# Attention of two heads in pairs of PSUM banks, with new priorities

## The chip, the cores and the metric

One core of a Trainium2 chip. The metric is the device time in microseconds of one execution; the shown figure before is the median of three runs, 772.94 us. PE is TensorE, DVE VectorE, ACT ScalarE, POOL GpSimd, SP SyncE, whose queue issues all the transfers. PSUM, into which PE writes, has eight banks of 512 float32 columns.

## What is computed

Attention over 4 batches of 8 heads, 576 positions of 64 numbers, in two parts that are added: a coarse one (q, k and v averaged over four positions) and a local one (each position sees those less than four away). Then two feed-forward layers over the 4 x 576 tokens of 512 numbers. Cut from the reference:

```python
q_d, k_d, v_d = (t.reshape(B, H, S // 4, 4, D).mean(axis=3) for t in (q, k, v))
out_up = np.repeat(sm_attn(q_d, k_d, v_d), 4, axis=2)
mask = np.abs(pos[:, None] - pos[None, :]) < 4
out_local = softmax(where(mask, q @ k.T / 8, -1e9)) @ v
x = (out_up + out_local)                      # [B, S, 512]
xk, xr = mu_k * x + (1 - mu_k) * x_prev, mu_r * x + (1 - mu_r) * x_prev
x = sigmoid(xr @ w_r) * ((relu(xk @ w_k) ** 2) @ w_v)
x = x + relu(layernorm(x) * g_ln @ w_ch1) @ w_ch2
```

## The kernel before, in words

Attention goes by units: a unit is one batch and two neighbouring heads, 16 in all, four for a batch. Both heads lie one under the other in the 128 partitions (64 each), so that a unit gives 128 features of the array xT, from which the first layer reads. The function `attention(n, T0, TL)` adds a unit's operations to a list:

- Loads of k, q and v on SP's queue (`kin`, `qin`, `vw`, `v4`); q and k are transposed on DVE or, in units with a mode other than 0, on PE (`tq`) with an evacuation by ACT. `qd`, `kd`, `vd` are sums over four positions.
- Local scores `sc` (L623, L629): for each of the two heads one matmul that writes the mask into a bank, then 24 small matmuls (64 rows, 32 columns of the array; the trace shows two instructions for each). The head h lies in rows 64h to 64h+63. DVE takes the maximum (L640) and subtracts it (L643), ACT takes the exponential.
- Coarse scores `ds` (L655), in which the two heads alternate; their maximum on DVE, three exponentials on ACT.
- Sums, reciprocals and products on DVE; a 32x32 transpose to `pT` and four copies into the block matrix `PT`.
- `tp` (L707): six transposes of the coarse weights, in two tiles of one bank, each evacuated by ACT or DVE (L711, L712).
- `up` (L718): the coarse result, evacuated to `ups`.
- `pv` (L748): the local result in two halves of 288 positions, each a tile of one bank; DVE adds `ups` and writes xT (L762).

The first layer runs over six chunks of 384 tokens: `moe_r` (`psr`, sigmoid), `moe_k` (`psk`), `accumulate` (`psv`). The second runs over three pairs of chunks (`psh`, `pso`). Each float32 product is three matmuls (L778 to L780) of a high and a low part. The weights come as 64-bit numbers; two passes on ACT (L395, L397) and two on DVE (L402, L406) turn each 128x512 piece into float32, then a copy and a subtraction split it.

The order on each engine comes from the planner (`Plan.order`): all operations have a cost and a priority, and at every step it issues what can start earliest by its own simulation, the lower priority first among those. The priorities come from the table PRM. Where PE would stand before the first `psv`, the planner puts in warm-up matmuls (L433, tile `warm`) that compute nothing. A tile takes its bank when its first operation is issued and gives it back after its last. Tiles of one tag take turns in the order of their first operation.

Banks before: `ps_v` has three single banks (pv0, pv1, pv2; pv2 also holds the warm-ups), `ps_k` a ring of two, `ps_a` a ring of three. The function `psa` gives a bank to an attention tile: in batch 0 in turn from all three pools, later from the ring of three. In the second layer, `pso` uses all six of `ps_v` and `ps_a`.

A unit's work begins at priority T0, which for the first four is ta + u0 x n + t_n; loads of q and k have T0 - ld, loads of v ldv more. Loads of weights have the priority of their conversion less wld; for w_r that is wr + wrs x kt, for the first half of w_k wka + wkas x kt (kt from 0 to 3).

Of the kernel before, what the change touches and what calls it, by code (L numbers as in the profile page):

```python
# [9 lines left out]
F32 = mybir.dt.float32  # L10
# [14 lines left out]
    thin=89.915, t0=-16.294, t1=-9.875, t2=6.158, t3=7.667, t4=48.796, t5=19.99, t6=6.382, t7=-23.592, t8=-0.47,  # L25
    t9=-5.238, t10=-2.702, t11=0.12, t12=5.747, t13=-8.176, t14=-15.681, t15=-4.758, m0=2, m1=1, m2=0, m3=3, m4=1,
    m5=0, m6=0, m7=2, m8=3, m9=0, m10=0, m11=0, m12=0, m13=0, m14=0, m15=0, g0=0, g1=0, g2=0, g3=0, g4=0, g5=0, g6=0,
    g7=0, g8=0, g9=0, g10=0, g11=0, g12=0, g13=0, g14=0, g15=0, h0=1, h1=1, h2=1, h3=1, h4=0, h5=0, h6=0, h7=0, h8=0,
    h9=0, h10=0, h11=0, h12=0, h13=0, h14=0, h15=0, dve=0.27, pool=0, ta=-14.632, u0=4.274, tl=26.492, tm=4222.228,
    ld=33.163, ldv=76.41, mu=-14.605, wr=-0.059, wrs=-31.134, wka=-33.615, wkas=7.94, wkb=12.502, wkbs=-165.286,  # L30
    wv=103.601, wvs=2.875, wld=0.932, d0=235.165, d1=108.349, d2=260.708, d3=463.399, d4=581.694, d5=82886.056,
    a1=13.725, a1s=43.62, a1l=52.7, a2=-1.632, a2s=26.831, a2l=56.61, a3=54.215, a3s=40.382, a3l=96.628, xr=-60.685,
    xrs=16.307, xk=22.171, xks=1.12, xrn=9, xrns=1.512, xkn=-4.695, xkns=17.37, w2a=10.707, w2as=1.55, w2=7.281,
    w2s=34.846, wc=10.079, wcs=106.739, m2q=8, sld=-6.173, x1=3, wcg=-39.001, p0l=11.872, p0=2.352, p0s=3.263,
    p0n=7.723, dp=684.729, ra0=-8.097, ra1=-1.757, ra2=3.642, ra3=4.616, ra4=-5.44, ra5=0, rb0=0.342, rb1=19.209,
    rb2=16.653, rb3=33.463, rb4=10.116, rb5=0, rx0=-2.918, rx1=-13.421, rx2=8.601, rx3=12.062, rx4=-2.926, rx5=5.409,
    ne=12, we=52.842, wes=25.704, wel=6.378,
# [23 lines left out]
class Plan:  # L61
# [61 lines left out]
    def order(self):  # L123
# [17 lines left out]
        for k in sorted(range(nb), key=lambda k: first[k], reverse=True):  # L141
            turn[tag[k]].append(k)
# [123 lines left out]
def attn_moe_kernel(  # L266
# [175 lines left out]
    n_ps = [0]  # L442

    def psa(b, name):
        if b > 0:
            return Buf(ps_a, [P, 512], F32, "pa", 3, name)
        ring = [(ps_a, "pa", 3), (ps_k, "pk", 2), (ps_v, "pv0", 1), (ps_a, "pa", 3), (ps_k, "pk", 2),
                (ps_a, "pa", 3), (ps_v, "pv1", 1)]
        pool, tag, n = ring[n_ps[0] % len(ring)]
        n_ps[0] += 1  # L450
        return Buf(pool, [P, 512], F32, tag, n, name)

    def attention(n, T0, TL):
# [19 lines left out]
        join = PRM[f"g{n}"]  # L473
# [143 lines left out]
        for h in range(2):  # L617
            sc = psa(b, "sc")

            def score(h=h, sc=sc):  # L620
                if first:
                    warm_up(2)
                nc.tensor.matmul(sc()[:, :G * 32], identb, maskb.rearrange("p g c -> p (g c)"),  # L623
                                 start=True, stop=False)
                for g in range(G):
                    for j in range(4):
                        i = 4 * g + j
                        m = min(32, S - QB * i)
                        nc.tensor.matmul(  # L629
                            sc()[32 * j:32 * j + m, 32 * g:32 * g + 32],  # L630
# [5 lines left out]
            add("PE", 0.8 + hold(2), pr(0.2), score, r=[qT, kT], w=[sc] + held, thin=True)  # L636
            mx = Buf(at, [P, G, 1], F32, "mx", 2)
# [60 lines left out]


        pdT = Buf(at, [HS, 2, 2, SD], F32, "pdT", 1)  # L700
        for kt in range(2):
            tp = psa(b, "tp")
            tpv = lambda tp=tp: tp()[:HS, :2 * SD].rearrange("p (h c) -> p h c", c=SD)

# [598 lines left out]
```

## Time and profile before

| | us |
|---|---|
| runs (3) | 769.48, 772.94, 774.14 |
| median | 772.94 |
| the profiled execution | 771.95 |
| its span, first to last instruction | 770.2 |
| PE busy | 753.6 (98%) |
| DVE busy | 524.6 (68%) |
| ACT busy | 398.2 (52%) |

The granted clock of PE is 0.999 of full speed over the whole span. A busy PE in this table counts overlapping matmuls once, and counts warm-ups as well. Busy shares are means over stages with different limits, so the kernel is to be read by stage: 0 to 57 us (attention of batch 0, up to the first product), 57 to 235 us (attention of the batches 1 to 3 between products of the first layer), 235 to 387 us (first layer), 387 us to the end (second layer).

### The profile page before, as it was taken

What the parts mean: (1) busy time and instruction counts of PE and PEld (TensorE: products, weight loads), DVE (VectorE), ACT (ScalarE), POOL (GpSimd) and SP (SyncE); (2) the same over time, 40 slices, a digit from 0 to 9 for tenths busy, and PEclk for the clock granted to TensorE, in tenths of its full rate; (3) what the DMA queues carried; (4) which work ended last, traced back from release to release, by engine and by line L of the source; (5) the groups of instructions that cost most, each with busy time, mean ns of one, the idle gap of its engine ahead of it and who ended that gap; (6) DMA issues with size and microseconds to landing.
All of it is one profiled execution on the core that took longest, in us unless ns stands there. A gap on an engine that the chain in (4) does not pass through costs nothing.

```text
span 770.2 us, 15665 instructions
## 1 busy us (share of the span) xinstructions
PE 753.6 (98%) x5816; PEld 650.2 (84%) x5816; DVE 524.6 (68%) x1083; ACT 398.2 (52%) x916; POOL 63.8 (8%) x113
## 2 busy tenths in 40 slices
PE   9999999999999999999999999999999999999997
PEld 6878787788788798888888888889889899889886
DVE  6899999998985959878889763486543364333233
ACT  6889997987884847868835431221421131111110
POOL 3101122112100000000110000020000020000000
PEclk9999999999999999999999999999999999999999
DMA  8997596867768895964689894379853347443322
GB/s 190 208 192 180 180 180 124 182 170 144 207 159 267 251 323 171 290 217 135 141 281 289 208 258 121 112 246 305 183 150 115 112 121 258 138 120 113 123 69 82
DMA packets 202854, 140.88 MB, mean 183 GB/s; under 512 B 127120, under 2 KB 160028, under 8 KB 202780
## 3 DMA queue, kind: packets, MB, share of 16 engines
q1 hardware_dynamic: 202780, 139.90, 66.6%
q8 instruction: 46, 0.75, 0.4%
q14 instruction: 28, 0.23, 0.1%
HBM read 107.88 MB, written 31.98 MB: 182 GB/s over the span
## 4 chain that ended last, share of the span: by engine, by line
PE 77%; DVE 10%; DMA 6%; ACT 4%; issue 2%; POOL 0%; SPq 0%; DVEq 0%; POOLq 0%; ACTq 0%
PE pso L779 8%; PE pso L778 8%; PE pso L780 8%; PE psh L778 7%; PE psh L779 7%; PE psh L780 7%; PE psk L778 4%; PE psv L778 4%; PE psk L780 3%; PE psk L779 3%; PE psv L779 3%; PE psv L780 3%; DMA w<-in_moe_w_ch_dram 3%; PE warm L433 2%; DVE tmu L802 1%
## 5 line engine op out<-in xcount | busy, mean ns | idle before, releaser
L778 PE MATMUL psh<-xn,sa 128*128 128x384 f32 x336 | 114.0, 339 | 2.4 <-DVE c L1114 1.2
L779 PE MATMUL psh<-xn,sa 128*128 128x384 f32 x336 | 113.6, 338 | 0.0
L780 PE MATMUL psh<-xn,sa 128*128 128x384 f32 x336 | 113.3, 337 | 0.0
L778 PEld LDWEIGHTS psh<-xn,sa 128*128 128x128 f32 x336 | 63.1, 188 | 11.0 <-DVE c L1114 2.1
L779 PEld LDWEIGHTS psh<-xn,sa 128*128 128x128 f32 x336 | 63.1, 188 | 6.1 <-DVE xn L1051 0.2
L780 PEld LDWEIGHTS psh<-xn,sa 128*128 128x128 f32 x336 | 63.1, 188 | 0.0
L379 ACT ACTIVATE c22h<-t 128x384 fp32r<-128x384 f32 x24 | 12.6, 525 | 83.7 <-DVE t L1106 78.6
L395 ACT ACTIVATE wf<-w 128x512 f32<-128x512 f32 x48 | 32.3, 673 | 17.4 <-DMA w<-in_moe_w_ch_dram 9.2
L402 DVE SCALAR_TENSOR_TENSOR wf<-wf,w 128x512 uint32<-128x512 uint32 x48 | 32.9, 687 | 11.1 <-ACT w L397 10.6
L379 ACT ACTIVATE kr<-psk 128x384 f32<-128x384 f32 x46 | 22.4, 488 | 25.2 <-PE psk L780 21.2
L379 ACT ACTIVATE c11h<-psh 128x384 fp32r<-128x384 f32 x23 | 11.3, 491 | 45.8 <-PE psh L780 45.7
L397 ACT ACTIVATE w<-w 128x512 uint32<-128x512 uint8 x52 | 35.0, 672 | 0.0
L843 DVE TENSOR_TENSOR kl<-kr,kh 128x384 fp32r<-128x384 f32 x43 | 23.8, 553 | 14.6 <-ACT kr L842 14.3
L1083 DVE SCALAR_TENSOR_TENSOR c11l<-psh,c11h 128x384 fp32r<-128x384 f32 x24 | 13.3, 554 | 29.1 <-ACT c11h L379 29.1
L802 DVE SCALAR_TENSOR_TENSOR tmu<-xT,oms,tmu 128x384 f32<-128x384 f32 (+1 forms) x64 | 31.7, 512 | 1.8 <-ACT tmu L796 1.8
L406 DVE SCALAR_TENSOR_TENSOR wf<-w,wf 128x512 uint32<-128x512 uint32 x48 | 32.7, 680 | 0.3
L1106 DVE TENSOR_TENSOR t<-psh,t 128x384 f32<-128x384 f32 x24 | 13.3, 554 | 28.5 <-PE psh L780 28.4
L1097 DVE TENSOR_TENSOR u<-psh,u 128x384 f32<-128x384 f32 x24 | 13.3, 555 | 27.2 <-PE psh L780 27.1
L379 ACT ACTIVATE c12h<-c 128x384 fp32r<-128x384 f32 x24 | 12.6, 525 | 37.0 <-DVE c L1110 36.9
L379 ACT ACTIVATE c21h<-c 128x384 fp32r<-128x384 f32 x24 | 12.6, 523 | 34.6 <-DVE c L1114 34.6
L796 ACT ACTIVATE tmu<-xT,vecs 128x384 f32<-128x384 f32 (+1 forms) x51 | 26.8, 539 | 6.9 <-DVE xrl L806 4.0
L1103 DVE TENSOR_TENSOR t<-psh,u 128x384 f32<-128x384 f32 x24 | 13.2, 552 | 20.2 <-PE psh L780 20.1
(527 smaller groups left out, 2164.5 us busy)
## 6 DMA issues: line engine op xcount, KB each, us to landing
sa<-s_dram SPq DMA_DIRECT2D x168, 256.0 KB, 2.7
w<-in_moe_w_ch_dram SPq DMA_DIRECT2D x32, 512.0 KB, 6.2
s_dram<-s SPq DMA_DIRECT2D x56, 256.0 KB, 4.0
vw<-in_v_dram SPq DMA_DIRECT2D x62, 96.0 KB, 4.0
x_dram<-r SPq DMA_DIRECT2D x18, 256.0 KB, 3.4
x1t<-x_dram SPq DMA_DIRECT2D x6, 768.0 KB
z_dram<-x1t SPq DMA_DIRECT2D x18, 256.0 KB, 2.7
zb<-z_dram SPq DMA_DIRECT2D x96, 48.0 KB, 2.8
```

The source lines that it names most:

```text
L379: return [("ACT", c_act(n, True), lambda: nc.scalar.activation(dst(), src(), AF.Relu), False), ("DVE", c_dve(n), lambda: nc.vector.tensor_ ...
L395: add("ACT", c_act(512), prio, lambda: nc.scalar.activation(f(), w64().bitcast(F32)[:, :, 1], AF.Abs, scale=2.0 ** -112), r=[w64], w=[f])
L397: add("ACT", c_act(512), prio, lambda: nc.scalar.activation(w64()[:, :, 0], w64().bitcast(U8).rearrange("p a (b c) -> p a b c", c=4)[:, :, ...
L402: lambda: nc.vector.scalar_tensor_tensor(fu(), fu(), 3, w64()[:, :, 0], op0=ALU.logical_shift_left, op1=ALU.bitwise_or),
L406: lambda: nc.vector.scalar_tensor_tensor(fu(), w64()[:, :, 1], 0x80000000, fu(), op0=ALU.bitwise_and, op1=ALU.bitwise_or),
L433: nc.tensor.matmul(warm()[:, :304], identb, isumb, start=True, stop=True)
L778: nc.tensor.matmul(ps, lh, rh, start=start, stop=False, skip_group_check=more)
L779: nc.tensor.matmul(ps, lh, rl, start=False, stop=False, skip_group_check=more)
L780: nc.tensor.matmul(ps, ll, rh, start=False, stop=stop, skip_group_check=more)
L796: add([("ACT", c_act(n, ap=1), lambda t=t, o=o, n=n, cur=cur, kt=kt: nc.scalar.mul(t()[:, o:o + n], cur(), mu[:, kt:kt + 1]), False), ("DV ...
L802: lambda t=t, o=o, n=n, prv=prv, kt=kt: nc.vector.scalar_tensor_tensor(t()[:, o:o + n], prv(), om[:, kt:kt + 1], t()[:, o:o + n], op0=ALU. ...
L843: add(either(C, lambda e: e.tensor_tensor(kl(), kr(), kh().bitcast(F32), op=ALU.subtract)), 0, prio, None, r=[kr, kh], w=[kl])
```

## The change

Attention's tiles become pairs of banks, `[P, 2, 512]`, so that both heads' scores, both halves of the values and both sets of transposes are one operation each on PE and one on the engine that reads them.

- Scores: one operation writes both masks, then goes over the 24 positions with both heads alternating; head h writes bank h of the pair. Maximum and subtraction on DVE are one instruction each over 384 elements (before, two over 192).
- Transposes: six as before, into two banks; one evacuation of 576 elements (before, two of 288).
- Values: all 12 products of both halves in one operation; one addition of 576 elements on DVE.
- Two small operations get POOL as a possible engine: the scaling of `mxd` (in place of DVE) and the addition of 1e-9 to `stat` (beside DVE).
- The banks: `ps_v` has a pair (`pv`) and a single one, `ps_k` two single ones, `ps_a` a pair (`pp`) and one single bank (`pa`). In batch 0, pairs alternate between `pv` and `pp`, single tiles take `pk`, `pk`, `pa` in turn. Later, every pair is `pp` and every single tile `pa`.
- The accumulators `psv` and `pso` become one pair and one single bank, in place of three single ones.
- The joined way (`join`), which no unit used, is taken out. Unit 1 goes from mode 1 to mode 3, in which PE also makes the sums of q and k; mode 4 of unit 4 does what mode 1 did.
- All priorities in PRM are other numbers. In `order`, a tie between tiles is broken by their number.

```diff
 PRM = dict(
-    ... t0=-16.294, t1=-9.875, t2=6.158, t3=7.667, ... m0=2, m1=1, m2=0, m3=3, m4=1, ...
-    ... ta=-14.632, u0=4.274, tl=26.492, ... ld=33.163, ldv=76.41,
-    ... wr=-0.059, wrs=-31.134, wka=-33.615, wkas=7.94, ... wld=0.932, ...
+    ... t0=-14.927, t1=-9.298, t2=-1.526, t3=9.098, ... m0=2, m1=3, m2=0, m3=3, m4=4, ...
+    ... ta=10.407, u0=-3.022, tl=18.319, ... ld=72.162, ldv=81.744,
+    ... wr=-13.311, wrs=-43.356, wka=15.59, wkas=-25.771, ... wld=-24.516, ...
 ...
     def psa(b, name):
         if b > 0:
-            return Buf(ps_a, [P, 512], F32, "pa", 3, name)
-        ring = [(ps_a, "pa", 3), (ps_k, "pk", 2), (ps_v, "pv0", 1), (ps_a, "pa", 3), (ps_k, "pk", 2),
-                (ps_a, "pa", 3), (ps_v, "pv1", 1)]
+            return Buf(ps_a, [P, 512], F32, "pa", 1, name)
+        ring = [(ps_k, "pk", 2), (ps_k, "pk", 2), (ps_a, "pa", 1)]
 ...
+    def psp(b, name):
+        pool, tag = (ps_v, "pv") if b == 0 and n_ps[1] % 2 else (ps_a, "pp")
+        n_ps[1] += 1
+        return Buf(pool, [P, 2, 512], F32, tag, 1, name)
 ...
-        for h in range(2):
-            sc = psa(b, "sc")
-            def score(h=h, sc=sc):
-                if first:
-                    warm_up(2)
-                nc.tensor.matmul(sc()[:, :G * 32], identb, maskb.rearrange("p g c -> p (g c)"),
+        sc = psp(b, "sc")
+        def scores():
+            if first:
+                warm_up(2)
+            for h in range(2):
+                nc.tensor.matmul(sc()[:, h, :G * 32], identb, maskb.rearrange("p g c -> p (g c)"),
                                  start=True, stop=False)
-                for g in range(G):
-                    for j in range(4):
+            for g in range(G):
+                for j in range(4):
+                    for h in range(2):
                         nc.tensor.matmul(
-                            sc()[32 * j:32 * j + m, 32 * g:32 * g + 32],
+                            sc()[32 * j:32 * j + m, h, 32 * g:32 * g + 32],
                             qT()[64 * h:64 * h + 64, QB * i:QB * i + m],
                             kT()[64 * h:64 * h + 64, QB * i:QB * i + 32],
 ...
-            add("PE", 0.8 + hold(2), pr(0.2), score, r=[qT, kT], w=[sc] + held, thin=True)
+        add("PE", 1.25 + hold(2), pr(0.2), scores, r=[qT, kT], w=[sc] + held, thin=True)
 ...
-        add([("DVE", 0.2, lambda: nc.vector.tensor_scalar_mul(mxd()[:, 0:3], mxd()[:, 0:3], -0.0078125), False),
+        add([("POOL", 0.25, lambda: nc.gpsimd.tensor_scalar_mul(mxd()[:, 0:3], mxd()[:, 0:3], -0.0078125), False),
 ...
-        add("DVE", 0.18, pr(0.5), lambda: nc.vector.tensor_scalar_add(stat()[:, 0:15], stat()[:, 0:15], 1e-9),
-            w=[stat])
+        more = lambda e: (lambda: e.tensor_scalar_add(stat()[:, 0:15], stat()[:, 0:15], 1e-9))
+        add([("DVE", 0.35, more(nc.vector), False), ("POOL", 0.25, more(nc.gpsimd), False)], 0, pr(0.5), None, w=[stat])
 ...
-        for kt in range(2):
-            tp = psa(b, "tp")
+        tp = psp(b, "tp")
+        add("PE", 0.94, pr(0.65), tpose, r=[pd], w=[tp], thin=True)
 ...
-        for half in range(2):
-            pv = psa(b, "pv")
+        pv = psp(b, "pv")
+        def pvmm():
+            for g in range(G):
+                for hp in range(2):
+                    nc.tensor.matmul(
+                        pv()[64 * hp:64 * hp + 64, g // 3, 96 * (g % 3):96 * (g % 3) + 96],
+                        vw()[:, hp, g, :], PT[:, hp, g, :], start=True, stop=True)
+        add("PE", 1.4, pr(0.85), pvmm, r=[vw, PTb], w=[pv], thin=True)
+        add("DVE", c_dve(576), pr(0.9), ...)
 ...
+    def accs(pool, pair, one, name):
+        b2, b1 = Buf(pool, [P, 2, 512], F32, pair, 1, name), Buf(pool, [P, 512], F32, one, 1, name)
+        return [(lambda: b2()[:, 0], (b2, 0)), (lambda: b2()[:, 1], (b2, 1)), (b1, b1)]
 ...
-        pvs[c] = [Buf(ps_v, [P, 512], F32, f"pv{t}", 1, f"psv{t}") for t in range(TT)]
+        pvs[c] = accs(ps_v, "pv", "pv2", "psv")
 ...
+                    pv = accs(ps_v, "pv", "pv2", "pso") + accs(ps_a, "pp", "pa", "pso")
```

## Rows read from the trace of the kernel before

**Rows 1.** The page, span and section 1: busy time, share of the span, instructions.

```profile
span 770.2 us, 15665 instructions
PE 753.6 (98%) x5816; PEld 650.2 (84%) x5816; DVE 524.6 (68%) x1083; ACT 398.2 (52%) x916; POOL 63.8 (8%) x113
```

**Rows 2.** Windows by stage: busy us of each engine (instructions), clock, DMA share, GB/s.

```profile
0.00:57.00 57.00, 52.89 (x943) 41.14 (x947) 46.16 (x109) 42.62 (x116) 9.27 (x38) 1.00 1.00 196
57.00:235.00 178.00, 174.69 (x2318) 142.78 (x2305) 162.94 (x357) 151.17 (x391) 30.75 (x56) 1.00 0.73 169
...
387.00:770.00 383.00, 377.17 (x1863) 336.69 (x1861) 193.64 (x377) 94.05 (x187) 15.14 (x12) 1.00 0.56 170
```

**Rows 3.** Windows of the warm-up matmuls (L433) alone: PE and weight-load busy us.

```profile
0.00:57.00 57.00, 21.55 (x128) 11.78 (x128) 1.00 1.00 196
```

**Rows 4.** The chain that ended last, 0 to 60 us: start, us, what.

```profile
1.78 4.69 PE warm L433 x24
...
28.66 1.31 PE vs L604 x12
...
45.61 6.70 DMA w<-in_moe_w_r_dram
```

**Rows 5.** Who made PE wait, 57 to 235 us: total, times, longest.

```profile
PE psk L778 <- ACT r L822: 1.5, 1, 1.5
PE tp L707 <- DVE xT L762: 0.4, 1, 0.4
PE up L718 <- DVE pdT L712: 0.4, 1, 0.4
```

**Rows 6.** Timeline of PE, a unit's scores: start, us, engine, line, tiles, shapes.

```profile
157.72 0.26 PE L623 MATMUL sc<-maskb,identb 128*128 128x192 bf16 x1
...
158.46 0.26 PE L623 MATMUL sc<-maskb,identb 128*128 128x192 bf16 x1
158.64 0.61 PE L629 MATMUL sc<-kT,qT 64*32 64x32 f32 x48
159.19 0.34 PE L718 MATMUL up<-pdT,vd 72*64 72x144 f32 x2
```

**Rows 7.** Timeline of all engines, 57 to 173 us: other operations of units.

```profile
57.31 0.49 PE L778 MATMUL psr<-wr0h,xrh 128*128 128x512 f32 x1
...
160.97 0.31 DVE L643 TENSOR_TENSOR e<-sc,mx 128x192 f32<-128x192 f32 x1
...
162.12 0.95 PE L655 MATMUL ds<-kd,qd 64*64 64x144 f32 x12
...
163.00 1.21 PE L748 MATMUL pv<-PT,vw 128*64 128x96 f32 x24
...
164.14 0.50 PE L778 MATMUL psv<-wv2h,kh 128*128 128x512 f32 x1
...
165.41 0.45 DVE L762 TENSOR_TENSOR xT<-pv,ups 128x288 f32<-128x288 f32 x1
...
168.44 0.26 PE L623 MATMUL sc<-maskb,identb 128*128 128x192 bf16 x1
...
172.07 0.82 PE L707 MATMUL tp<-isum,pd 128*72 128x128 f32 x6
...
172.60 0.74 ACT L711 ACTIVATE pdT<-tp 72x288 f32<-72x288 f32 x2 [0.16 <-PE tp L707]
```

**Rows 8.** Groups by line, engine, shape: count, busy us, mean ns, idle before.

```profile
L762 DVE TENSOR_TENSOR xT<-pv,ups 128x288 f32<-128x288 f32 x32 | 13.8, 443 | 1.0 <-PE pv L748 0.9
L640 DVE TENSOR_REDUCE mx<-sc 128x6 f32<-128x192 f32 x32 | 10.9, 346 | 1.0 <-PE sc L629 0.7
...
L677 DVE TENSOR_REDUCE stat<-e 128x12 f32<-128x384 f32 x16 | 8.6, 537 | 0.2 <-ACT e L646 0.2
L679 DVE TENSOR_SCALAR stat<-stat 128x15 f32<-128x15 f32 x16 | 4.0, 248 | 0.2 <-ACT pd L673 0.2
```

**Rows 9.** Transfers issued in the first 57 us: operation, count, KB, us to landing.

```profile
w<-in_moe_w_k_dram SPq DMA_DIRECT2D x6, 512.0 KB, 5.7
```

More of the change, by code (lines that the diff above doesn't have):

```diff
@@ L24 @@
 PRM = dict(
[L25 to L34, printed above, removed]
@@ new lines @@
+    m5=0, m6=0, m7=2, m8=3, m9=0, m10=0, m11=0, m12=0, m13=0, m14=0, m15=0, g0=0, g1=1, g2=1, g3=0, g4=0, g5=1, g6=1,
+    g7=0, g8=1, g9=0, g10=0, g11=0, g12=0, g13=0, g14=0, g15=0, h0=1, h1=1, h2=1, h3=1, h4=0, h5=0, h6=0, h7=0, h8=0,
+    h9=0, h10=0, h11=0, h12=0, h13=0, h14=0, h15=0, dve=0.27, pool=0, ta=10.407, u0=-3.022, tl=18.319, tm=164.109,
+    ld=72.162, ldv=81.744, mu=1.003, wr=-13.311, wrs=-43.356, wka=15.59, wkas=-25.771, wkb=5.259, wkbs=-21.824,
+    wv=109.639, wvs=3.182, wld=-24.516, d0=276.014, d1=218.841, d2=538.006, d3=427.467, d4=1012.653, d5=1567441.483,
@@ L38 @@
+    rx4=-7.207, rx5=36.576, ne=12, we=53.115, wes=25.808, wel=7.39,
 )
@@ L140, in order @@
         turn = {t: [] for t in slots}
-        for k in sorted(range(nb), key=lambda k: first[k], reverse=True):
+        for k in sorted(range(nb), key=lambda k: (first[k], k), reverse=True):
             turn[tag[k]].append(k)
@@ L723, in upper @@
                     )
-        if not join:
+        if True:
             up = psa(b, "up")
@@ new lines, in attention @@
+        pv = psp(b, "pv")
[6 more added lines that the diff above has]
+        add("PE", 1.4, pr(0.85), pvmm, r=[vw, PTb], w=[pv], thin=True)
+        add("DVE", c_dve(576), pr(0.9),
+            lambda: nc.vector.tensor_tensor(
+                x()[:, u, 1:1 + S].rearrange("p (f s r) -> p f s r", f=2, r=4),
+                pv()[:, :, :288].rearrange("p f (s r) -> p f s r", r=4),
+                ups().rearrange("p (f s) r -> p f s r", f=2).to_broadcast([P, 2, 72, 4]),
+                op=ALU.add), r=[pv, ups], w=[(x, (u, 0)), (x, (u, 1))])
@@ L1254, in attn_moe_kernel @@
                 if f == 1:
-                    pv = [Buf(*((ps_v, [P, 512], F32, f"pv{n}", 1) if n < TT else (ps_a, [P, 512], F32, "pa", 3)), f"pso{n}")
-                          for n in range(2 * TT)]
+                    pv = accs(ps_v, "pv", "pv2", "pso") + accs(ps_a, "pp", "pa", "pso")
                 for k_, n in enumerate((3, 4, 5, 0, 1, 2)):
@@ L1270, in attn_moe_kernel @@
             o.deps.add(gate.writer[None])
-    plan.issue(lambda: warm_up(1), 0.14, pvs[0][2])
+    plan.issue(lambda: warm_up(1), 0.14, pvs[0][2][0])
 _INS = ['q', 'k', 'v', 'moe_mu_k', 'moe_mu_r', 'moe_w_k', 'moe_w_v', 'moe_w_r',
```

93 lines of the change are left out of this document (32 added, 61 removed).

## The prediction

> **What bounds the kernel now.** I read the page first, then the windows by stage, then who made TensorE wait, and last the chain and the timeline. The page shows TensorE (PE) busy for 753.6 of 770.2 us [rows 1]. The windows by stage split this: in the first 57 us attention of batch 0 and the first weights' conversion run, and PE is filled up with warm-up matmuls; from 57 to 235 us attention of the other three batches (12 units of two heads) runs between MoE products; after 387 us the second product runs, with PE at 377 of 383 us and VectorE (DVE) at only 194 [rows 2].
>
> The reader is to see three different limits. In the first 57 us, 21.55 us of PE's time are warm-up matmuls that compute nothing [rows 3], DVE is busy for 46.2 us and the DMA engines for all of it [rows 2]; the chain that ended last runs through a weight load of 6.70 us [rows 4]. So this stretch ends when data is there, not when PE is done. From 57 to 235 us PE is at 174.7 of 178 us, DVE at 162.9 and ACT at 151.2 [rows 2]. What PE waits for there is a few single events: 1.5 us once for a sigmoid buffer, and 0.4 us twice at attention operations [rows 5]. PE sets the end there, and DVE stands close behind it. After 235 us no operation is changed, save which bank an accumulator lies in. A microsecond of PE work saved between 57 and 235 us is therefore a microsecond of the whole, as long as DVE and the banks keep pace.
>
> **The change, part by part.** *Scores.* Today one head's scores take 0.73 us from one mask matmul to what follows it, the pair 1.47 us (157.72 to 159.19): 0.18 us for a mask, then 0.55 us for 48 small matmuls, all in one 64-row half of the array [rows 6]. The new order alternates the halves. No row shows 64x32 matmuls alternating. The nearest is the downsampled score, which does alternate halves: 12 matmuls of 144 columns in 0.88 us (162.12 to 163.00) [rows 7], 0.51 ns a column, while matmuls on the whole array take 1.31 us for 12 of 128 columns, 0.85 ns a column [rows 4]. Alternating thus costs 0.6 of one after another. For scores: 2 x 0.55 x 0.6 = 0.66, with two masks 0.36, 1.02 us; 0.45 us saved in each unit. The bounds: nothing saved, if these are already as dense as PE starts them (11 ns each); or the second 0.55 gone entirely, 0.91 us, 0.56 saved. That alternating loses time is excluded by the downsampled scores. I take 0.45: in 12 units 5.4 us (0 to 6.7). In the four units of the first 57 us I count nothing, since warm-ups fill the hole there.
>
> The Trainium skill (TensorE: Matmul & The Clock Gate, Part 3) says that tiles of different row groups run concurrently about 4 ns apart, and that a weight load passes a matmul in flight only when the row group differs. By it 96 matmuls would take an estimated 0.38 us, 0.74 with the masks, and the sum would be 3.4 us lower than by my 0.66. The trace agrees on overlap and shows no spacing of 4 ns; its present scores are 11 ns apart [rows 6]. A rule against the change stands in the Trainium skill (TensorEngine Tiling (Array Packing), Instruction Overhead): about 60 cycles for every matmul however few its columns. By it pairing could give nothing, and the sum would be 5.4 us higher; the trace disagrees already, at 11 ns for each.
>
> *Values and transposes.* Two value halves now come back to back as 24 matmuls in 1.14 us (163.00 to 164.14) [rows 7] where units did so before; the change makes it so always. I count 0.5 us for the few units in which they stood apart (0 to 1). The transposes are the same six matmuls; nothing.
>
> *VectorE and ACT.* One pass over twice the elements in place of two. A DVE reduction takes 346 ns over 192 elements and 537 over 384 [rows 8], so a second instruction costs about 0.15 us beyond its elements. Maximum and subtraction, which pass over the same elements, 4 x 346 = 1.38 us, become about 2 x 0.54 = 1.08; the addition of the two parts 2 x 443 = 0.89 becomes 443 + 288 x 1.0 ns = 0.73. That is 0.45 us in a unit, 0.70 if the 248 ns of the small addition also go to POOL; 5.4 to 8.4 us in 12 units. The transposes' evacuation loses a start of 0.16 us or so on ACT. All of this costs or gives nothing between 57 and 235 us as long as PE is the bound (162.9 against 174.7 busy); if PE's stretch shrinks by 6 us and DVE's by as much, they keep their distance. In the first 57 us, where DVE is 81% busy, four units give 1.8 to 2.8 us; I take 1.5 (0 to 2.8), because the chain also runs through DMA.
>
> *The banks.* Instead of three single banks the later batches get one pair and one single bank. Scores, transposes and values of every unit go through the one pair, downsampled scores and the upper part (and, in units 4, 7 and 8, four q/k transposes each) through the one single bank: 12 x 5 + 12 = 72 handovers, each one a place where PE can stand, with all MoE matmuls queued behind it, and DVE and ACT after these. How long is the pair held? By today's times 157.72 to 161.28 for scores, 163.00 to 165.86 for values, 172.07 to 173.34 for transposes, 7.7 us together, while the next unit's scores begin 10.72 us after this one's [rows 6, 7]. That fits, without much room. Bounds of the price: nothing, if the planner puts enough MoE matmuls between them (it books the evacuation), or the whole evacuation, two passes of 0.54 us, about 1 us at each of 72. Today's waits at attention operations with three banks are 0.4 + 0.4 us [rows 5], each the only one of its kind; with one slot of each kind I take two and a half times that, 2 us, being nearer to this row than to the other end.
>
> *Priorities.* They decide which ready operation goes first, and can't be costed by rows of instructions. One part can be read: before, the four loads of the first half of w_k have priorities (wka + wkas x kt - wld) of -34.5 to -10.7 and stand ahead of all value loads of batch 0 (T0 - ld + ldv, 12.3 to 49.1); after, two of the four stand at 14.3 and 40.1, with value loads from 5.1 to 20.0. Six such loads of 512 KB are issued in the first 57 us [rows 9] at 196 GB/s [rows 2], 2.7 us each, on full DMA engines. w_k isn't needed until the sigmoid products are through. If two loads leave the stretch, at most 5.4 us do; I take 3 (0 to 5.4). Unit 1 also gets its q and k sums from PE, where PE has warm-ups to replace; nothing.
>
> *Sum.* -5.4 - 0.5 - 1.5 - 3 + 2 = -8.4 us against the profiled execution's 771.95 (770.2 span and 1.75 around it): 763.6. The median of the runs is 1.0 us above that execution, so I forecast 764.
>
> **The rivals.** *The pair of banks becomes the bound.* For it: held 7.7 of 10.7 us, and DVE, which has to free it, is 92% busy in this stretch, its queue in order. Against it: PE has MoE matmuls to put between, and present waits are small. The gains are 10.4 us; at a mean wait of 0.14 us at the 72 handovers they are gone, from about 0.25 us (18 us) the kernel is more than 1% slower. Time: 780 to 785. The Trainium skill (TensorEngine Tiling (Array Packing), PSUM Bottleneck) warns that evacuation, which tiling doesn't speed up, may become the limit; the trace of before shows no such wait of size [rows 5]. Chance 0.14.
>
> *The scores don't get faster and the start stays.* Matmuls 11 ns apart may be held by their issue and not by their half of the array; then 5.4 us fall away, and if data sets the first 57 us as now, 3 more. 772. For it: 48 matmuls in 0.55 us is already far below 0.85 ns x 32 columns = 27 ns each. Against it: they overlap over column groups, which leaves the other half of the rows idle. Chance 0.21.
>
> *More comes from the start than I count.* Of the first 57 us PE spends 21.55 on warm-ups [rows 3]; 4.69 of these stand at the very beginning, before anything has landed [rows 4]. If new priorities bring the first product forward by 10 us in place of 4.5, and scores pair at their lower bound (1.3 us more), the time is 757; with some waits avoided later, 752. For it: DMA is the limit there and some of its traffic can wait. Against it: w_k is wanted a few us later, and 0.73 of the DMA time is in use then as well [rows 2]. Chance 0.20. The spacing that the Trainium skill gives (above) would lead to the same end by another way, 3.4 us lower than my sum, 760.
>
> **How the numbers follow.** My forecast gets 0.45, with 758 to 769 as its own range. About 1% (7.7 us) is what a measurement of this kernel can tell from no change; that bound lies at 765.2, and I put 0.31 of the 0.45 below it. Faster: 0.31 + 0.20 = 0.51. Same: 0.14 + 0.21 = 0.35. Slower: 0.14. The range is to leave out 0.1 on each side: half of the fast rival below 752, most of the slow one above 778.
>
> **What would show it.** Right: the score matmuls of a pair span about 1.0 us with masks; DVE has 16 instructions each for maximum and subtraction at 0.54 us; the first sigmoid product starts at 52 to 54 us instead of 57.3 [rows 7]; the last attention unit ends earlier than now by about that and 4 us more; PE's waits at scores, transposes and values stay below 3 us in all. Wrong: a pair still takes 1.4 us; first product at 57 us or later; waits of PE for the maximum's, transposes' or final addition's reader at 20 or more places; DVE alone full while PE stands, or waits after 235 us, where I count none, since a changed order shifts weight conversions into it.

## The result, and the profile after

The changed kernel takes 781.58 us (median of four runs, 780.08 to 783.32) against 772.21 us for the kernel before on the same chip: a ratio of 1.0125, with a 95% interval of 1.0083 to 1.0167. It is slower by 9.4 us, where 764 us had been forecast. The profiled execution of it took 783.32 us, 11.4 us more than the 771.95 us that the prediction's sum started from. Ratios, here and below, are of fast runs alone; only in e11 is there a slow run, which stands in its median and not in its ratio.

| | before | after |
|---|---|---|
| median of the runs, us | 772.21 | 781.58 |
| profiled execution: time / span, us | 771.95 / 770.2 | 783.32 / 781.5 |
| first sigmoid product (`psr`) starts, us | 57.3 | 51.5 |
| first `psr` of the second chunk, us | 127.0 | 134.3 |
| first product of the second layer (`psh`), us | 380.4 | 389.3 |
| last matmul, us | 765.9 | 777.5 |

The last four lines tell the story. At the first `psr` the changed kernel is 5.8 us ahead, as hoped. At the first `psr` of the second chunk it is already 7.3 us behind. By the second layer it is 8.8 us behind, so 14.6 us are lost on the way, and the second layer adds 2.8. The last attention unit ends at 236.3 us, where it ended at 233.9.

The page, span and busy time (to be held against [rows 1]):

```profile
span 781.5 us, 15602 instructions
PE 757.8 (97%) x5826; PEld 652.1 (83%) x5826; DVE 517.1 (66%) x1002; ACT 398.6 (51%) x906; POOL 81.1 (10%) x143
```

The windows by stage (busy us of PE, weight loads, DVE, ACT, POOL; then the granted clock, the DMA share, GB/s):

```profile
0.00:57.00 57.00, 54.05 (x871) 42.81 (x872) 43.16 (x89) 40.19 (x107) 11.64 (x42) 1.00 0.97 187
57.00:235.00 178.00, 167.40 (x2329) 134.34 (x2327) 157.34 (x295) 148.24 (x379) 44.34 (x80) 0.97 0.75 171
...
387.00:770.00 383.00, 379.69 (x1874) 338.40 (x1873) 197.12 (x387) 101.35 (x203) 18.11 (x15) 1.00 0.56 168
```

Against [rows 2]: between 57 and 235 us PE is busy for 7.3 us less (167.40, was 174.69), DVE for 5.6 less and ACT for 2.9 less. None of the three is fuller than before, and less comes out: they stand more, and the lists below show for whom. The granted clock of the stretch is 0.97, where it was 1.00.

Who made PE wait, 57 to 235 us (total, times, longest), in the changed kernel:

```profile
PE up L722 <- DVE pdT L716: 3.2, 1, 3.2
PE tq L566 <- ACT kT L371: 2.0, 1, 2.0
PE tq L563 <- ACT kd L371: 1.6, 1, 1.6
PE sc L636 <- issue: 1.0, 1, 1.0
PE pv L743 <- ACT pdT L715: 0.7, 1, 0.7
PE tp L711 <- ACT pdT L715: 0.7, 1, 0.7
PE sc L628 <- ACT pdT L715: 0.4, 1, 0.4
PE tp L711 <- DVE xT L749: 0.3, 1, 0.3
PE tp L711 <- DVE e L648: 0.3, 1, 0.3
```

That is 10.2 us at nine places, against 3.0 us at six before (the three longest are [rows 5]). Seven of the nine are waits for a place, by the releasers that the profile names: `tq`, `pv`, `tp` and `sc` stand until ACT or DVE has copied the previous tile out of the one single bank or the one pair, 6.0 us together. The wait of 1.0 us inside a scores operation (180 us) has no releaser in the profile ("issue"), and its cause is open. The first in the list is a wait for data: the `up` product needs pdT. The timeline of PE shows it and what comes behind (start, us, instruction; in brackets the idle time before and who ended it):

```profile
84.98 0.40 PE L767 MATMUL psv<-wv1h,kl 128*128 128x512 f32 x1
88.60 1.23 PE L722 MATMUL up<-pdT,vd 72*64 72x144 f32 x8 [3.22 <-DVE pdT L716]
89.75 1.50 PE L711 MATMUL tp<-isum,pd 128*72 128x128 f32 x6
91.99 2.19 PE L743 MATMUL pv<-PT,vw 128*64 128x96 f32 x24 [0.74 <-ACT pdT L715]
93.96 1.17 PE L722 MATMUL up<-pdT,vd 72*64 72x144 f32 x8
```

And the windows around it (columns as above):

```profile
80.00:85.00 5.00, 5.00 (x29) 4.29 (x27) 5.00 (x9) 4.81 (x16) 1.66 (x3) 1.00 0.47 153
85.00:88.00 3.00, 0.37 (x2) 0.00 (x0) 2.92 (x7) 2.38 (x6) 1.39 (x2) 0.96 0.36 111
88.00:98.00 10.00, 8.67 (x54) 6.32 (x56) 8.34 (x16) 8.47 (x21) 0.99 (x1) 0.50 0.83 194
98.00:108.00 10.00, 10.00 (x185) 8.28 (x185) 7.92 (x15) 5.76 (x17) 0.40 (x3) 1.00 0.98 183
```

PE stands for 3.22 us while DVE works almost without a gap (2.92 of 3.00 us), and the granted clock, 1.00 until then, is 0.50 from 87.8 to 98.0 us: PE runs at 1.2 GHz and not at 2.4. Later units of the changed kernel show the same blocks at full clock, and a pair's scores:

```profile
162.43 0.71 PE L722 MATMUL up<-pdT,vd 72*64 72x144 f32 x8
163.07 0.34 PE L628 MATMUL sc<-maskb,identb 128*128 128x192 bf16 x2
163.34 1.01 PE L636 MATMUL sc<-kT,qT 64*32 64x32 f32 x96
164.28 0.95 PE L659 MATMUL ds<-kd,qd 64*64 64x144 f32 x12
...
166.93 1.32 PE L743 MATMUL pv<-PT,vw 128*64 128x96 f32 x24
```

At full clock `up` costs 0.71 us, `tp` 0.82 ([rows 7]) and `pv` 1.32, so the four blocks at half clock, 1.23 + 1.50 + 2.19 + 1.17 us, lose 2.5 us beyond the wait itself. Before, no stretch between 4.7 and 769 us had a lower clock.

Last, the timeline of PE near the end:

```profile
769.13 0.39 PE L767 MATMUL pso<-w27h,c12l 128*128 128x512 f32 x1
770.30 0.50 PE L765 MATMUL pso<-w215h,c22h 128*128 128x512 f32 x1 [0.78 <-DVE res L1130]
...
774.35 0.39 PE L767 MATMUL pso<-w27h,c11l 128*128 128x512 f32 x1
775.52 0.50 PE L765 MATMUL pso<-w215h,c21h 128*128 128x512 f32 x1 [0.79 <-DVE res L1130]
```

PE writes one half of an accumulator pair, DVE reads the other half, and PE waits for the reading. A matmul that follows its neighbour by 0.23 us elsewhere follows it here by 1.17: 0.94 us lost, three times in the run, and never before the change. The planner books the two halves as independent of each other (`(b2, 0)` and `(b2, 1)` in the change), so its order doesn't allow for this wait.

### The profile page after: what moved, and what is told of

Same layout as the page of the kernel before. It is cut to its first block, busy times and chain, and to the rows that moved or that the text cites. A ratio compares the mean times of both kernels' runs of the same rounds, so it can differ in the third digit from the quotient of the medians.

```text
span 781.5 us, 15602 instructions
## 1 busy us (share of the span) xinstructions
PE 757.8 (97%) x5826; PEld 652.1 (83%) x5826; DVE 517.1 (66%) x1002; ACT 398.6 (51%) x906; POOL 81.1 (10%) x143
## 4 chain that ended last, share of the span: by engine, by line
PE 73%; DMA 9%; DVE 7%; ACT 7%; issue 2%; SPq 1%; POOL 0%; DVEq 0%; ACTq 0%; POOLq 0%
PE pso L765 8%; PE pso L766 8%; PE pso L767 7%; PE psh L765 7%; PE psh L766 6%; PE psh L767 6%; DMA w<-in_moe_w_ch_dram 4%; PE psv L765 3%; PE psk L765 3%; PE psv L767 3%; PE psv L766 3%; PE psk L767 3%; PE psk L766 3%; PE warm L433 2%; DMA w<-in_moe_w_k_dram 1%
## 5 line engine op out<-in xcount | busy, mean ns | idle before, releaser
L379 ACT ACTIVATE kr<-psk 128x384 f32<-128x384 f32 x44 | 21.5, 488 | 20.6 <-PE psk L767 15.7
L1043 POOL TENSOR_TENSOR xn<-raw,xn 128x384 fp32r<-128x384 f32 x13 | 15.3, 1186 | 138.5 <-ACT xn L375 81.4
```

The lines of the kernel that those rows point to most:

```text
L379: return [("ACT", c_act(n, True), lambda: nc.scalar.activation(dst(), src(), AF.Relu), False), ("DVE", c_dve(n), lambda: nc.vector.tensor_ ...
```

## The experiments

Thirteen kernels ran, each beside the kernel before on the same chip. "Order kept" means that the planner's order is computed first, as in the named kernel, and the edit is made afterwards, so that every engine's queue stays as it was.

| kernel | median, us | ratio to before (95%) |
|---|---|---|
| the changed kernel | 781.58 | 1.0125 (1.0083 to 1.0167) |
| e1 new structure, old priorities | 783.83 | 1.0177 (1.0120 to 1.0234) |
| e2 old structure, new priorities | 792.02 | 1.0271 (1.0242 to 1.0300) |
| e3 accumulators apart | 777.96 | 1.0102 (1.0054 to 1.0150) |
| e4 heads in turn | 785.60 | 1.0182 (1.0145 to 1.0218) |
| e5 pdT on ACT, order kept | 784.41 | 1.0162 (1.0124 to 1.0201) |
| e6 after, DVE lighter, order kept | 781.28 | 1.0110 (1.0060 to 1.0160) |
| e7 before, DVE lighter, order kept | 770.16 | 0.9974 (0.9956 to 0.9992) |
| e8 before with two banks, planned anew | 782.58 | 1.0136 (1.0104 to 1.0168) |
| e9 before, alternating, order kept | 772.76 | 1.0008 (0.9993 to 1.0023) |
| e10 before, alternating, planned anew | 776.38 | 1.0060 (1.0040 to 1.0079) |
| e11 before with two banks, order kept | 801.93 | 1.0351 (1.0320 to 1.0383) |
| e12 after, the wait filled, order kept | 779.00 | 1.0109 (1.0046 to 1.0171) |
| e13 apart and filled | 775.20 | 1.0044 (1.0021 to 1.0068) |

### Structure or priorities: e1 and e2

e1 is the changed kernel with the whole PRM of the kernel before; e2 is the kernel before with the new PRM (its `g` entries at 0, so that the joined way stays off).

> The changed kernel with the whole table of priorities (PRM) of the kernel before; pairs of banks, alternating scores and paired accumulators stay. Theory P (the new priorities lose the time: their order rests on bookings that the chip doesn't keep, 3 us in the first 15 us and a stall of PE of 3.4 us at 85 us with 10 us of halved clock behind it): 766 to 771 us, since 0.25 us of PE time in each of 16 units is kept and the stall goes; only the three waits of 0.94 us at paired accumulators remain. Theory B (one pair and one single bank make PE stand, whatever the priorities): 777 us or more, with waits at scores, transposes and values over 5 us between 57 and 235 us.

> The kernel before with the priorities and modes of the changed kernel (joined way off, so that the operations are those of before). Theory P: slower than before, 776 us or more, with the lag in the first 15 us (first scores' successors 3 us later than booked) seen here too. Theory B: 769 to 774, since three banks take up what the order gets wrong, and the first sigmoid product still starts 4 to 6 us earlier than 57.3 us.

Measured: 783.83 us (777.75 to 787.77) and 792.02 us. e2 is slower than both kernels. e1 is slower than the kernel before, but its interval doesn't tell it apart from the changed kernel. Neither theory holds in full: e1's time is that of theory B, but its waits at scores, transposes and values are 2.4 us and not over 5; e2's time is that of theory P. The first sigmoid product starts at 59.8 us in e1 and at 62.7 in e2, later than the 57.3 of before, so the changed kernel's 51.5 needs both halves of the change.

The planner's own end, worked out with `order` from each kernel's operations, is 767.6 us before, 764.5 for the changed kernel, 767.2 for e1 and 778.4 for e2. The planner thus holds the changed kernel for 3 us faster. The chip runs 4.6 us above the plan before, 17.1 in the changed kernel, 16.6 in e1 and 13.6 in e2. What is lost is not in the plan, under either set of priorities; in e2 that holds without the pairs, so a new order alone can open such a gap too.

The new structure loses 11.7 us even with the old priorities, and the new priorities lose 20 us with three single banks. Undoing the whole set of priorities at once tells little about one part: it draws a new order for all engines. The later runs therefore keep the order where they can.

### The accumulators: e3

```diff
-for k_, n in enumerate((3, 4, 5, 0, 1, 2)):
+for k_, n in enumerate((3, 0, 5, 4, 1, 2)):
```

The last products go into the six accumulators in an order in which no two halves of a pair follow each other, and they are read out in the same order.

> The changed kernel, but the second layer's accumulators are filled and drained in the order 3, 0, 5, 4, 1, 2 in place of 3, 4, 5, 0, 1, 2, so that the two halves of a pair of banks are no longer neighbours in time. If the three waits of PE for the final addition (0.94 us each, at 527, 769 and 774 us) come from the other half of the same pair being read, they vanish: 2 to 3 us less than the changed kernel's 781.6, and at the end of the trace the matmuls run through. If they have another cause (the bank's turn, the result buffer), they stay and the time is that of the changed kernel.

Measured 777.96 us, 3.6 less than the changed kernel. Waits of PE for `res` are gone from its list in the second layer, and the last third of that layer, from its first `psh` to the last matmul, takes 134.0 us as in the kernel before (136.4 in the changed one). The last two thirds take 259.7 us in the traces of before, e2, e3, e7 to e11 and e13, and 263.1 or 263.2 us in those with the pair and its old order (the changed kernel, e1, e4, e5, e6, e12). Who made PE wait in e3's second layer, 392 to 780 us:

```profile
PE psh L765 <- DVE c L1106: 2.0, 2, 1.2
PE psh L765 <- ACT u L371: 0.3, 1, 0.3
...
```

The cause is shown, and its size: 3.4 of the 9.4 us, more than a third of the loss, are the pair of accumulators. In e3's own trace the second layer as a whole is only 1.7 us shorter, since its first third, with the waits for `c` above, takes 126.8 us (125.1 in the changed kernel).

### The alternation itself: e4 and e9

e4 takes the pairing of the scores' matmuls out of the changed kernel; e9 puts it into the kernel before, with three single banks and the order kept, in the 14 of 16 units whose two scores stand next to each other on PE. In e4 both heads' scores remain one operation, with both masks first.

```diff
 # e4, in the changed kernel
-for g in range(G):
-    for j in range(4):
-        for h in range(2):  # matmul(sc[:, h, ...])
+for h in range(2):
+    for i in range(4 * G):  # matmul(sc[:, h, ...])
 # e9, in the kernel before: two single banks t[0], t[1]
+for g in range(G):
+    for j in range(4):
+        for h in range(2):  # matmul(t[h][...])
```

> The changed kernel, but the 24 small score matmuls of head 0 come before those of head 1 instead of alternating; same order of operations, same bookings, same banks. If alternating gives the 0.25 us by which a pair's scores are shorter now (1.21 against 1.46 us), they take 1.46 us again. If PE is the bound between 57 and 235 us, the time is 3 to 4 us longer than the changed kernel's; if PE stands there anyway for others' data, it is within 1 us.

> The kernel before with its three banks and its order of operations kept; where the two heads' scores of a unit stand next to each other on PE (14 of 16 units) their matmuls alternate between the heads, in two single banks, so that the first reduction waits for both heads. If the alternation is worth on PE what it was in the changed kernel (0.25 us a unit), and neither places nor order are lost, the time falls by 1 to 3.5 us, to 768.5 to 771 us. If the later reduction gives it back, it stays within 1 us of 772 or rises.

Measured: e4 785.60 us, 4.0 more than the changed kernel; e9 772.76 us, 1.2 more than its 771.59 us of before, an interval that spans no change (0.5 us less to 1.8 more). A unit's scores in e4, one head after the other:

```profile
101.51 0.34 PE L628 MATMUL sc<-maskb,identb 128*128 128x192 bf16 x2
101.78 1.01 PE L636 MATMUL sc<-kT,qT 64*32 64x32 f32 x96
102.72 0.45 PE L765 MATMUL psk<-xkh,wk11h 128*128 128x384 f32 x1
```

They take 1.21 us (101.51 to 102.72), and 1.21 to 1.22 in the 13 of 16 units that hold no wait. That is the changed kernel's time (163.07 to 164.28); 1.46 had been expected. So alternating the halves saves PE nothing. The 0.25 us come from joining the two heads into one operation: the masks stand behind each other (0.27 us, where each had 0.18), and the 96 small matmuls are one stretch of 0.94 us and not two of 0.55. In the traces each such stretch ends with 0.12 us before the next matmul starts, which one stretch pays once.

e4's 4.0 us are therefore not the length of its scores. Its profiled execution has waits of 1.5 and 3.7 us inside two scores operations (181.5 and 192.4 us), without a releaser in the profile, and half clock from 190.5 to 197.4 us; the changed kernel has 1.0 us and full clock there. Why they are longer is open; e3 and e6 have such waits too (2.2 and 1.7 us).

In e9 the saving on PE is there: the two masks and the 96 small matmuls of one unit,

```profile
158.56 0.34 PE L624 MATMUL sc<-maskb,identb 128*128 128x192 bf16 x2
158.83 1.01 PE L631 MATMUL sc<-kT,qT 64*32 64x32 f32 x96
159.77 0.71 PE L747 MATMUL up<-pdT,vd 72*64 72x144 f32 x8
```

take 1.21 us (158.56 to 159.77), where [rows 6] had 1.47. The reduction that waits for them does not come sooner: it starts at 159.90 us, 1.34 after the scores began; before, it started at 159.02, 1.30 after (157.72). DVE has other work in its queue until then:

```profile
158.91 0.55 DVE L872 TENSOR_TENSOR kl<-kr,kh 128x384 fp32r<-128x384 f32 x1
159.38 0.55 DVE L835 TENSOR_TENSOR xrl<-tmu,xrh 128x384 fp32r<-128x384 f32 x1
159.90 0.36 DVE L669 TENSOR_REDUCE mx<-sc 128x6 f32<-128x192 f32 x1
```

So in the kernel before 14 x 0.25 = 3.5 us of PE's work, eleven of the units and 2.8 us from 56 us on, are worth nothing, and PE's waits between 57 and 235 us rise from 3.0 to 4.8 us. This is not PE's work alone: the first head's maximum, which could start after its own scores, now has to wait for both heads.

### Who sets the pace: e5, e6, e7

After the first runs the theory was that DVE sets the pace from 60 to 90 us, since it works there without a gap and its pdT comes late. e5 lets ACT make the three pdT that DVE made; e6 and e7 shorten the two DVE operations that join a weight's bits, 24 in the changed kernel and 26 in the one before, from 512 to 64 columns (the other columns of those weights stay unjoined).

```diff
 # e5, after the order is set
+if len(o.ways) == 2 and o writes pdT: o.way = 0
 # e6, e7
-scalar_tensor_tensor(fu(), fu(), 3, w64()[:, :, 0], ...)
+scalar_tensor_tensor(fu()[:, :cut()], fu()[:, :cut()], 3, w64()[:, :cut(), 0], ...)
+cut = lambda: 64 if 50 < Plan.now < 120 else 512
```

> The changed kernel with its instruction order kept, in which the three copies of pdT that stood on DVE stand on ACT at the same place (two at the start and the one of 87.7 us, 0.74 us; ACT did the other nine). Theory D (DVE sets the pace between 60 and 90 us, its pdT comes 3.2 us late, PE stands, and the granted clock then falls to 0.5 for 10.2 us): the stall before `up` at 85 us shrinks below 2 us, no clock of 0.5 between 87 and 98 us, and the time falls by 3 to 6 us, to 775.5 to 778.5 us. Theory B (it is the two banks: the same time is lost at the next handover): within 1.5 us of the changed kernel's 781.6 us.

> The changed kernel, order kept, in which the two DVE operations that put an 8-byte weight's bits together work on 64 columns rather than 512 wherever they are booked between 50 and 120 us (24 of them, so those weights are wrong): about 0.43 us each taken from DVE, 10 us together, and nothing else. Theory D (DVE sets the pace there): the first psr of the second chunk comes 5 to 10 us earlier and the whole time falls by 6 to 12 us, to 770 to 776 us. Theory B (waits for banks and for ACT set it): less than 3 us.

> The kernel before, order kept, with the same 26 operations on 64 columns (11 us taken from DVE). If PE sets the end between 57 and 235 us, as the prediction had it, the time stays within 2 us of 772. If DVE sets the pace in the kernel before too, it falls by 4 to 8 us, to 764 to 768 us.

Measured 784.41, 781.28 and 770.16 us. The theory falls twice. With 10 us less for DVE the changed kernel gains 0.3 us (1.2 by the ratios; the interval allows up to 5). The wait before `up` shrinks to 1.7 us, and half clock comes all the same, from 91.0 to 97.9 us. With pdT on ACT the stall is no shorter, since ACT's queue is late too:

```profile
88.18 1.09 PE L724 MATMUL up<-pdT,vd 72*64 72x144 f32 x8 [3.38 <-ACT pdT L717]
```

The kernel before gains 2.2 us for 11 us of DVE's work: neither PE (e9) nor DVE (e7) sets its end alone. Two rivals stay untested: no run lightened ACT, and none the loads of weights. In the chain that ended last, loads of `w_ch` alone are 7.8% of the time from 57 to 235 us before and 13.2% after. That the chain goes from engine to engine through the banks is argued here; the next runs test the banks.

### Places: e8, e10, e11

e8 gives the attention of batches 1 to 3 two single banks in turn, in the kernel before, and lets the planner set the order. e11 does the same with the order kept. e10 is the control: the order set anew (for the alternation of e9, in all units), with all three banks.

```diff
-return Buf(ps_a, [P, 512], F32, "pa", 3, name)
+return Buf(ps_a, [P, 512], F32, "pa", 2, name)
 ...
```

The cut part gives the third bank to some tiles of batch 0 and to one accumulator of the second layer.

> The kernel before, in which the attention of batches 1 to 3 has two single PSUM banks in turn rather than three (the third holds only the last accumulator of the second layer). Nothing is merged. Theory B (fewer places for a result cost the most): 777 to 785 us. Theory D (three banks or two hardly matter, since DVE sets the pace): 771 to 775 us.

> The same alternation in all 16 units, with three banks, but the planner sets the order anew with a booked cost of 1.25 us (it books an end 1.6 us later than for the kernel before). Theory B (places): no place is lost, so 767 to 773 us. Theory R (any order other than the one the priorities were set for loses several us on the chip, with the same banks too): 775 to 780 us.

> The kernel before with its order of operations kept, in which the attention of batches 1 to 3 has two single banks in turn rather than three: the same instructions in the same order, and only the waits for a free bank are new. Theory B (places): slower by 5 us or more, 777 to 790 us, with waits of scores, transposes and values for the copies that free a bank. Theory R (the replanned order costs, not the waits): 771 to 775 us.

Measured 782.58, 776.38 and 801.93 us. With nothing merged, nothing alternated and no operation added, two places in place of three cost 27 us by the ratio (25 to 30) if the order stays, and 10.2 us (782.58 against 772.37) if the planner may arrange itself with them; its plan books 5.7 of these. An order set anew with three banks costs 4.8 us (776.38 against 771.59), of which its plan books 1.7. So some 3 to 5 of the 10 may be the new order as such; the rest goes with the missing bank. Not all of it is lost between 57 and 235 us: in e8 the first `psr` is already 3.7 us late (61.0, before 57.3). And e11's price has the clock in it: its profiled execution runs 17 us at half clock, which is up to an estimated 8.5 us. e11's list of who made PE wait, 57 to 235 us, is what the prediction had been afraid of:

```profile
PE sc L629 <- ACT pd L679: 6.9, 2, 4.6
PE pv L754 <- DVE xT L768: 2.1, 3, 0.9
PE sc L629 <- DVE e L649: 1.7, 1, 1.7
PE tp L713 <- ACT pdT L717: 1.1, 2, 0.6
PE pv L754 <- DVE ups L373: 1.0, 1, 1.0
PE up L724 <- DVE e L649: 1.0, 1, 1.0
...
```

and more, 20 us at 23 places. Nearly all are scores, values, transposes or upper parts behind the reader of the tile that has the bank.

### The stall and the clock: e12 and e13

e12 puts 22 matmuls that nobody reads, 2.8 us together, ahead of the `up` block of 85 us, into the bank that the block overwrites. pdT comes no sooner for it; PE only doesn't stand. e13 adds the order of e3.

```diff
 def upper():
+    if 84 < Plan.now < 85:
+        for _ in range(22):
+            nc.tensor.matmul(up()[:, :304], identb, isumb, start=True, stop=True)
```

> The changed kernel, order kept, in which 22 matmuls that nobody reads (304 columns, 0.129 us each, 2.8 us together) go ahead of the one `up` block that waits 3.2 us for pdT at 85 us, into the bank that the block is about to overwrite. Nothing becomes ready earlier. Theory C (the stall costs little by itself, the clock of 0.5 that follows it for 10.2 us costs more): no clock of 0.5 between 85 and 98 us, and 3 to 6 us less than the changed kernel's 781.6, so 775.5 to 778.5. Rival (the clock of 0.5 falls where other engines set the pace and costs nothing): 780 to 783 us.

> The same filling, in the version whose accumulators are taken in the order 3, 0, 5, 4, 1, 2 (778.0 us without it). Theory C, with the gains adding up: 772 to 775 us, no slower than the kernel before by more than 3 us. Rival: 776.5 to 779 us.

The windows of e12 around the stall, and below them the last two of e13:

```profile
85.00:88.00 3.00, 3.00 (x23) 2.13 (x22) 2.92 (x6) 2.38 (x6) 1.39 (x2) 1.00 0.28 86
88.00:98.00 10.00, 8.50 (x97) 6.20 (x95) 9.81 (x18) 9.25 (x23) 1.55 (x1) 1.00 1.02 215
```

```profile
88.00:98.00 10.00, 8.80 (x184) 6.88 (x183) 9.78 (x19) 8.87 (x24) 1.70 (x3) 1.00 1.05 202
98.00:108.00 10.00, 9.96 (x165) 7.56 (x166) 8.25 (x17) 6.87 (x16) 1.57 (x2) 1.00 1.09 166
```

The granted clock stays at 1.00 where it had been 0.50. The median of e12 is 779.00 us, 2.6 less than the changed kernel and 0.5 above what theory C expected; its interval is wide, since its profiled execution fell to half clock after other waits (for 3.4 us from 113.5 and 6.8 us from 195.4) and took 787.25, while the other three, with a mean clock of 1.0, took 775.62 to 780.92. e13 took 775.20 us (770.48 to 777.35, ten runs), 2.8 less than e3, whose only difference is the filling, and 6.4 less than the changed kernel (6.3 by the ratios). That 2.6 and 2.8 agree is chance in part: held against the kernel before of the same chip, by the ratios, the two pairs give 1.2 and 4.5 us, and neither interval alone rules out that the filling is worth nothing. Shown is that the clock of the stretch stays at 1.00 in both, and that both edits together take back 6.3 of the 9.4 us. The times speak for theory C, but what the filling alone is worth is not settled.

## Why the prediction was wrong, step by step

- **The start came out right, its grounds are not shown.** First `psr` at 51.5 us, forecast 52 to 54; in sum -4.5 us forecast for DVE's merges and the weight loads, -5.8 measured. But the merges alone (e1, 59.8 us) and the new priorities alone (e2, 62.7) both start later than before. Of the six loads of w_k in the first 57 us two left, as forecast, and one of w_v took a place there. That the two terms add up is luck in part.
- **DVE's merged instructions were right in size:** maximum 546 ns and subtraction 536 (forecast 540). DVE's total fell by 7.5 us. Its worth was overestimated everywhere behind the start: e6 and e7.
- **The scores: "Alternating thus costs 0.6 of one after another" failed.** A pair takes 1.21 us, not 1.02: 0.25 us saved and not 0.45, in 12 units 3.0 us and not 5.4. And the 0.25 us are not the alternation's: e4's pairs, without it, take 1.21 to 1.22 us. At 32 columns the 96 matmuls of one pair start 9.8 ns apart (163.34 to 164.28), and 9.9 in e4, against 11 before in two stretches. The second rival had said that they may be held by their issue and not by their half of the array: not by their half is shown, what holds them is not. The ratio came from the downsampled scores with 144 columns, held against matmuls that the prediction took for the whole array; they use 72 of its columns (`128*72` in the trace). The Trainium skill's 4 ns (TensorE: Matmul & The Clock Gate, Part 3) is not reached, and its 60 cycles for each (TensorEngine Tiling (Array Packing), Instruction Overhead) are not seen.
- **"PE sets the end there" failed, and this is the step that counts most.** It was read from a busy share of 98% and waits of 3.0 us. In the changed kernel PE is busy for 7.3 us less in the stretch and the second layer starts 8.8 us later. In the kernel before, e9 takes 3.5 us of PE's work away and the time stays; e7 takes 11 us from DVE and gets 2.2. With PE, DVE and ACT at 175, 163 and 151 of 178 us a microsecond saved on one is not a microsecond of the whole. That the end is set by a chain through all three fits this; whether ACT or the weight loads lead it was not tested.
- **The banks were mis-sized: +2 us.** In the profile 6.0 us of waits for a place stand in the stretch, where comparable ones were 0.6 before. That isn't all of it: a wait holds up PE's queue, DVE and ACT get their input later, and the 3.22 us wait for pdT is one that no list of places holds. The prediction looked for a small wait at each of 72 handovers, and for 20 or more places as a sign of being wrong; what came were few long ones. Two other signs did come: DVE full while PE stands (2.92 of 3.00 us from 85 us), and waits after 235 us. The longest for a place (2.0 and 1.6 us) stand at `tq`, the transposes of q and k, which the prediction named in its count and gave no price of their own. e11 prices one bank in three in the kernel before: 27 us with its order kept, 10 us in e8 with a new one. That number could not be read from the waits before, because three banks are what kept them small.
- **The clock was left out.** A stall of 3 us costs more than 3 us: 2.5 us more on the four blocks behind it. Filling the wait kept the clock at 1.00; how much time it gets back is not settled (1.2 and 4.5 us by the ratios).
- **"Where I count none", after 235 us, failed.** The accumulators' pair was described in the change and costed at nothing, with the words "save which bank an accumulator lies in". It costs 3 x 0.94 us in waits and 3.4 us over the last two thirds of the layer, in every run that has it.
- **The rival that came true** is the first, the pair of banks as the bound, 780 to 785 us, with a chance of 0.14. Its place was right and its mechanism only in part: with the accumulators apart and the one stall filled (e13) 6.3 of the 9.4 us are gone, and neither was a wait at one of its 72 handovers.
- **A slip of the sum:** -8.4 us from the median of 772.94 is 764.5, not 764. Nothing hangs on it.

What remains, 3.8 us (e13 against before, interval 1.6 to 5.2), stands although the start is 6 us earlier and the scores shorter. From PE's first matmul to the second layer's first, PE is idle for 8.5 us before, 13.9 after and 9.9 in e13. Warm-ups and the 22 fillers take 20.0, 20.6 and 22.7 us there, and the matmuls that compute 350.1, 353.0 (with the half clock) and 348.5. So e13 computes 1.6 us less than the kernel before, and stands or fills for 4.1 us more: what remains is waiting. That it comes from two places in place of three is argued from e8 and e11 and not shown, since no run gave the changed kernel a third place; how much of it is the new order, as in e10, stays open.

Both heads' scores, 2 x 192 columns, would fit side by side in one single bank, which would save a place. That was not tried. The downsampled scores already alternate the row halves into one bank, each half into 64 partitions of its own; scores of both heads would share the partitions. The Trainium skill (TensorEngine Tiling (Array Packing), Gotcha 1: PSUM Pressure) says that different row tiles can't access one bank at the same time; no run here settles what that means for such a layout.

## What to carry to other kernels

Before operations are merged into wider tiles, count the places that are left to turn over, and price one place by taking it away from the kernel as it is (27 us here with the order kept, 10 with a new one); short waits in a profile show that there are enough places, not that one can be spared. Where three engines are each more than 80% busy in one stretch, test on the chip what an engine's microsecond is worth there before it goes into a sum: 3.5 us of PE and 11 us of DVE were worth 0 and 2.2. Before a saving is put down to a mechanism, undo that mechanism alone: e4 shows that the shorter scores owe nothing to the alternation. When two accumulators share a tile, let the reader of one half and the writer of the other not follow each other. Where TensorE has a long stall that can't be removed, filling it is worth a try: here it kept the clock at 1.00.

## What the runs showed of the hardware

The granted clock is the surprise. In the changed kernel and in e3 to e6 every period of half clock between the start and the end follows a stall of PE of 1.6 to 3.7 us that ended, or was still going on, when the clock fell: 3.22 us behind the matmul of 85.0, then 0.50 from 87.8 to 98.0; in e8 2.54 us behind that of 28.3, then 0.50 from 33.0 to 36.4. It does not follow every such stall: 1.97 us behind the matmul of 58.6 in the changed kernel and 2.74 us behind that of 192.1 in e5 left the clock at 1.00, and in e11 two periods follow stalls of only 0.8 and 1.0 us. The kernel before, with no wait over 1.5 us from 57 to 235 us, has none there. The Trainium skill (TensorE: Matmul & The Clock Gate, HAM oscillation — how this bites in real kernels) describes waits between bursts of matmuls after which the next burst starts slow; the trace agrees, 0.50 behind the stall and 1.00 with the same stall filled (e12).

A second one: the order of the small scores matmuls (64 rows, 32 columns) doesn't matter here. 96 of them take 0.94 us when the two row halves alternate and 0.94 to 0.95 when one half follows the other (e4).

A third: of the 16 additions of 1e-9 to `stat`, 248 ns each on DVE in the mean ([rows 8]), 15 went to POOL, where one takes 381 ns. DVE then waits four times for it, 2.2 us in all, before it can go on with the reciprocal; it had been spared 15 x 0.25 = 3.7 us. More than half of what the move to an idle engine saved the busy one came back as waiting.
